# Queries of one batch: from TensorE transposes to a crossbar DMA, and its scores later in the order

## The chip, the cores and the metric

The kernel runs on one core of one Trainium2 chip. The metric is device time in microseconds (us), from launch to end; smaller is better. A core has five engines with an instruction queue each: PE (TensorE, matrix products), DVE (VectorE), ACT (ScalarE), POOL (GpSimd) and SP (SyncE, which here only issues DMAs). An engine takes its instructions strictly in order, so one that waits holds up all behind it. Sixteen DMA engines move data for all of them. In a profile, PEld is PE's loading of weights, and SPq or POOLq is an engine's own queue of DMA issues.

## The reference

Two stages, on 8 batches of 8 heads, with 576 positions of 64 values in each head, and 32 memory slots.

```
a       = softmax(phi) over the 576 positions          # (8, 8, 576, 32)
k_m     = a^T k,   v_m = a^T v                         # 32 slots of 64 values per head
attn    = softmax(q k_m^T / sqrt(64)) over the 32 slots
x       = attn v_m, heads side by side                 # (4608, 512)
out     = (silu(x w_gate) * (x w_val)) w_out           # w_gate, w_val: 512 x 1536; w_out: 1536 x 512
```

Inputs and the output are fp32; the kernel works in bf16 with fp32 sums.

## The kernel before

**Tiling.** A batch is worked on as a whole. Its k and v come as one tile of 128 partitions (two heads side by side, 64 partitions each), its queries as a tile `t_q` of 128 x 2304, which has to be transposed, as 18 blocks of 128 x 128, into `t_qT` before scores can be made. `attn v_m` is never formed: `v_m` is multiplied into the gate and value weights (`U`, lines 453 to 492), and the attention `A` is multiplied by that (`gv_slots`).

**One batch.** Its steps are: exponentials of phi on ACT (`phi_exp`); sums over positions on PE (`kv_items`, L230), whose results DVE scales (`kv_norm`, L266, tile `t_bkv`) and which PE transposes (`kv_T`, L288), with a copy by DVE to `t_kT`; scores on PE (`scores`, L389), which need `t_kT` and `t_qT`, and their exponentials on ACT (L400); the sums of those on DVE (`z_inv_v`) and the scaling by them (`norm`); the products `U` (L465); 24 steps of a gate product, a value product, silu and a multiplication (L508, L525, L531), which give the hidden tile `t_h`.

**The last product.** `h w_out` is done with seven products in place of eight (`products`, line 682): sums and differences of blocks of `h` (tiles `t_S`, made by GpSimd or DVE, `chunk_done`) and of `w_out` (tiles `t_T`, made by DVE, `weight_sums`). A product is six units, and a unit is two matmuls of 128 x 256 (L720) into PSUM. The results are called `first` (12 units), `five`, `six`, `three`, `seven` and `four` (6 each). They share PSUM tiles: `three` adds to the tile of `five` after ACT has copied that out (`keep`, L745). Finished blocks are added up on DVE (L750), and SP stores them (`store_block`, L676).

**Order.** The order of the instructions on each engine is written by hand, as the order of the calls in the program. Batches 0 and 1 run first, while the weights arrive. Then a loop runs over batches 2 to 7. In it, a list `backlog` holds product units of the batch before, and `run(take(6))` puts six of them between two steps of the current batch. For batch 2, `zero` and `one` are the unit lists of batches 0 and 1.

**Queries.** Batches 0, 1 and 2 are transposed on PE (`q_items`, `q_T`, L376: six blocks to a PSUM tile, then a copy to `t_qT` by ACT, L330, or DVE). Batches 3 to 7 go through the crossbar of the DMA engines (`load_qT`, L117), issued by SP: for batch 3 at the head of the loop's first pass, for the later ones near the end of the pass before. `t_q` has two buffers, for even and odd batches; `t_qT` has two as well.

**Loads.** Nearly all loads are issued by GpSimd, between its own additions, and go through one queue in order. A load waits for the eighth load before it to have landed. The order around the change is: weights of the value side (L138), first and second third of `w_out` with k of 2 and phi of 2 between, last third of `w_out` (L153), v of 2 (L103). Then GpSimd makes the `t_S` sums of batch 0, first third, and after them issues phi of 3 and q of 2 (`beside_sums`, line 665); after the sums of batch 1, first third, q of 3; after the next, k and v of 3. `loads(4)` follows near 72 us.

The lines that the change touches, and those around them:

Of the kernel before, what the change touches and what calls it, by code (L numbers as in the profile page):

```python
# [14 lines left out]
def kernel(  # L15
# [19 lines left out]
    nc = tc.nc  # L35
# [39 lines left out]
    def bank(shape, dtype, name):  # L75
        tag = free.pop(0)
        t = ps.tile(shape, dtype, tag=tag, name=name)
        held[id(t)] = tag, t
        return t
# [8 lines left out]
    def head_pairs(x):  # L88

        return x.rearrange("h s d -> (h s d)").rearrange("(i p f) -> p i f", i=NP, p=128)  # L90

    def load_phi(b, eng):
        t = inp.tile([128, NP, JK * M], FP32, tag="phi", name="t_phi")
        eng.dma_start(out=t, in_=head_pairs(phi[b]))
        phis[b] = t
# [6 lines left out]
    def load_v(b):  # L102
        nc.gpsimd.dma_start(out=kvs[b][:, 1], in_=head_pairs(v[b]))  # L103

    def load_q(b):

        t = inp.tile([128, NS * 128], BF16, tag=f"q{Q_SLOT[b]}", bufs=1, name="t_q")
        nc.gpsimd.dma_start(  # L108
            out=t,
            in_=q[b].rearrange("h s d -> (h s d)").rearrange("(p f) -> p f", p=128),  # L110
        )
        qs[b] = t

    def load_qT(b):

        qTs[b] = att.tile([128, NS, 128], BF16, tag="qT", name="t_qT")
        nc.sync.dma_start_transpose(out=qTs[b], in_=qs[b])  # L117
# [33 lines left out]
    def load_wo(c):  # L151
        t = wpool.tile([128, 4, DM], BF16, tag=f"WO{c}", name=f"WO{c}")
        nc.gpsimd.dma_start(  # L153
            out=t,
            in_=moe_w_out[c * CH:(c + 1) * CH, :].rearrange("(i p) f -> p i f", p=128),
        )
        for i in range(4):
            WO[4 * c + i] = t[:, i]
        WOc[c] = t
# [62 lines left out]
    def kv_sum(b, p, parts):  # L222


        w0, w1 = parts[0], parts[-1] + 1
        n = (w1 - w0) * D
        for j in range(JK):
            for i in range(NP):
                for g in range(NG):
                    nc.tensor.matmul(  # L230
                        p[g][32 * i:32 * i + 32, 0:n],
                        lhsT=phi_of(b, g, j, i),
                        rhs=kvs[b][64 * g:64 * g + 64, w0:w1, i, j * D:(j + 1) * D],
                        start=(j == 0),
                        stop=(j == JK - 1),
                        tile_position=(64 * g, 32 * i),
                    )

    def kv_denominators(b, p):

        if b in masked:
            for g in range(NG):
                for j in range(JK):
                    nc.tensor.matmul(
                        p[:, g:g + 1],
                        lhsT=masked[b][:, j, g].rearrange("p i m -> p (i m)"),
                        rhs=ones1,
                        start=(j == 0),
                        stop=(j == JK - 1),
                    )  # L250
            return
        if b in esums:
            hl = esums.pop(b)
            terms = [hl[:, t] for t in range(2)]
        else:
            terms = [ephis[b][:, j].rearrange("p i m -> p (i m)") for j in range(JK)]
        for n, x in enumerate(terms):
            nc.tensor.matmul(p, lhsT=x, rhs=ones2, start=(n == 0), stop=(n == len(terms) - 1))
# [33 lines left out]
    def kv_items(b, beside=None):  # L292


        def run_sums():
            o = 2 * D
            p = [bank([128, CH], FP32, f"p_kv{g}") for g in range(NG)]
            behind = b in esums
            if not behind:
                kv_denominators(b, p[0][:, o:o + NG])  # L300
            kv_sum(b, p, (0, 1))
            if behind:
                beside()
                kv_denominators(b, p[0][:, o:o + NG])
            kv_reciprocal(b, p[0][:, o:o + NG])
            kv_norm(b, p)
            if beside and not behind:
                beside()

        return [run_sums, lambda: kv_T(b)]  # L310
# [329 lines left out]
    def quad_sums(qd):  # L640
# [22 lines left out]
                    subtract(nc.gpsimd, t[:, 2], A12, t[:, 1])  # L663

    beside_sums = {
        (0, 0): lambda: (load_phi(3, nc.gpsimd), load_q(2)),
        (1, 0): lambda: load_q(3),
        (0, 1): lambda: (load_k(3), load_v(3)),
    }
# [1 line left out]
    def store_block(t_o, b, n, cols):  # L671

        rows = out_r[b, n, 0:256, cols].rearrange("(u t) c -> t u c", u=2)
        parts = [slice(u, u + 1) for u in range(2)] if b < 2 else [slice(0, 2)]
        for u in parts:
            nc.sync.dma_start(out=rows[:, u], in_=t_o[:, u, cols])  # L676

# [144 lines left out]
    def q_items(b, evac):  # L822
        return [lambda n=n: q_T(b, n, evac[n]) for n in range(3)]
# [17 lines left out]
    def run(items):  # L841
        for x in items:
            x()
# [10 lines left out]
    def exp_tables():  # L854
        nc.scalar.preload_act_table_set("natural_log_exp_and_others")
# [50 lines left out]
    load_wo(1)  # L906
    load_phi(2, nc.gpsimd)
    load_wo(2)
    load_v(2)
    for c in range(NCH):  # L910
        u_buffer(1, c, f"S{c}")
# [55 lines left out]
    def take(n):  # L967
        nonlocal backlog
        n = max(0, min(n, len(backlog)))
        part, backlog = backlog[:n], backlog[n:]  # L970
        return part
# [17 lines left out]
    for b in range(2, B):  # L989
        last = b + 1 == B  # L990
        exp_tables()
        if b == 2:
            load_qT(3)
            phi_exp(2)
            (zero, ops0), (one, ops1) = products(0, ("c11",)), products(1, ("p1", "c11"))
            kv, q2 = kv_items(2), q_items(2, "aaa")
            run(zero[:6])
            sums = {n: f for n, f in zip(((1, 1), (0, 2), (1, 2)), late)}
            late.clear()
            sums[0, 2]()  # L1000
            weight_sums(0)
            weight_sums(1)
            run(zero[6:12] + one[:6] + kv[:1] + q2[:2])
            weight_sums(2, (0, 1))
            run(zero[12:16] + zero[18:22] + kv[1:] + q2[2:] + zero[16:18] + zero[22:24])
            weight_sums(2, (2, 3))
            ops0["c11"]()
            ops1["p1"]()
            wait_for(Ts[2][0:1, 3, 0, 0:1])
            for part in ((0, 1), (3,), (2,)):  # L1010
                for c in (1, 2):
                    sums[1, c](part)
            loads(4)
            backlog = one[6:12] + zero[36:] + one[12:36]
            ops = ops1
        else:
            run(take(6))
        for g in range(NG):
            scores(b, g)
        if b > 2:  # L1020
            ops["p1"]()
            u_values(b)
        else:
            run(zero[24:36] + take(6))
        run(take(6))
        z_inv_v(b, 0)
        ops["c11"]()
        run(take(6))
        if not last:
            phi_exp(b + 1)  # L1030
        z_inv_v(b, 1)
        if b > 2:
            norm(b, 0)
            norm(b, 1)
        run(take(6))
        run_late()
        if b == 4:
            wait_for(atts[4, 1][0:1, 0, 0:1])
            quad_sums(0)
        nc.scalar.preload_act_table_set("silu_and_others")  # L1040
        run(take(6))
        if b == 2:
            norm(2, 0)
        run(take(6))
        if b == 2:
            norm(2, 1)
            u_three(2)
            run(one[36:])
        g = gv_slots(b)
        quad = []  # L1050
        if b == 4:
            quad = products(b, (), 0)[0]
        if last:
            rest, rest_ops = products(b, (), 1)
            backlog += rest[:12]
        beside = 0 if last else 2 if quad else min(4, len(backlog))
        outs = [lambda: run(take(1)) for _ in range(len(backlog) - beside)]
        streams = [(g, 0, 24), (quad[:12], 0, 3), (quad[12:], 12, 18.5)]
        streams += [(outs, 4, 7 if quad else 24)]
        if b == 2:  # L1060
            streams += [([lambda: u_values(2)], 2.5, 3)]
        if last:
            streams += [([u_item(b, 2)], 5, 6)]
        if not last:
            if b > 2:
                load_qT(b + 1)
            if b > 2 and b != 4:
                phi_sum(b + 1)
            streams += [
                (kv_items(b + 1, lambda: (u_item(b, 2, "aava")(), run(take(2)))), KV, KV + 4),  # L1070
                ([lambda: (u_three(b + 1), run(take(2)))], 19, 20),
            ]
        spread(*streams)
        flush_mul()
        units, ops = products(b, ("p1", "c11"))
        backlog += units
# [34 lines left out]
```

The softmax here doesn't subtract the row's maximum and nothing guards it: scores larger than these inputs give would overflow.

## Time and profile before

| | |
|---|---|
| median of 3 runs | 233.49 us (233.4 to 233.51) |
| profiled execution, device time | 233.53 us |
| its span, first to last instruction | 231.7 us |
| PE, DVE, ACT, POOL busy | 222.8, 185.3, 171.7, 140.6 us |
| TensorE clock granted | 1.00 throughout |
| SP's 5 crossbar transposes of queries, issue to landing | 6.2 to 10.8 us, median 9.5 |
| q of 2: issued, landed | 42.70, 59.1 us |
| v of 2: issued, landed | 34.76, 54.3 us |
| q of 3: issued, landed | 48.20, 61.8 us |
| transposes of q of 2 on PE | from 59.13 and from 61.72 us |
| scores of 2, scores of 3 on PE | 63.11, 92.68 us |

The profile shows one execution. In a list of instructions the columns are start, length, engine, source line, operation, tile written <- tiles read, shape, count. In the chain of work that ended last they are start, length and what ran, followed back from the end. In a table of stretches, each engine's busy time is followed by its count of instructions, and the last three columns are the TensorE clock, the busy share of the DMA engines and the GB/s written. "To landing" is the time from a DMA's issue until its data is there.

### The profile page before, as it was taken

The page shows a single profiled execution, that of the slowest core. Times are in us where ns is not written, and L with a number is a line of the kernel's source. Part 1 is how long each engine was busy: PE and PEld are TensorE (multiplying, and loading weights), DVE is VectorE, ACT ScalarE, POOL GpSimd, SP SyncE. Part 2 cuts the span into 40 slices and gives each one's busy share as a digit, 9 for nine tenths or more (in the row PEclk, how much of TensorE's full clock was granted, in tenths as well). Part 3 has the DMA queues.
Part 4 walks back from the last instruction along what each step waited for, and adds up shares of the span by engine and source line. Part 5 has one row for each costly group of instructions (what it writes and reads, how often), then busy time and mean ns, then how long its engine had stood idle before and what let it go on. Part 6 is the DMA issues. An engine that isn't in the chain of part 4 may idle for free.

```text
span 231.7 us, 7206 instructions
## 1 busy us (share of the span) xinstructions
PE 222.8 (96%) x2825; PEld 169.9 (73%) x2825; DVE 185.3 (80%) x423; ACT 171.7 (74%) x365; POOL 140.6 (61%) x190
## 2 busy tenths in 40 slices
PE   7997899999999999999999999999999999999993
PEld 2554576778887776878788787887788778878882
DVE  4056789999966699989997668998999899977732
ACT  2858998988547889968896658978898789677310
POOL 8422427998199059765977689464845394039291
PEclk9999999999999999999999999999999999999999
DMA  6999999999997992999199945995013502202125
GB/s 211 210 211 205 199 207 207 219 247 269 203 205 197 260 254 44 227 212 183 54 218 193 235 131 104 249 237 102 22 71 106 112 0 95 91 6 88 29 87 160
DMA packets 36674, 36.84 MB, mean 159 GB/s; under 512 B 14624, under 2 KB 31008, under 8 KB 36640
## 3 DMA queue, kind: packets, MB, share of 16 engines
q0 software_dynamic: 16272, 22.42, 52.5%
q1 hardware_dynamic: 19600, 13.18, 22.9%
q10 hardware_dynamic: 768, 0.79, 1.1%
q8 instruction: 22, 0.36, 0.6%
q14 instruction: 12, 0.10, 0.1%
HBM read 42.47 MB, written 9.44 MB: 224 GB/s over the span
## 4 chain that ended last, share of the span: by engine, by line
PE 86%; DMA 9%; POOL 2%; ACT 1%; issue 0%; DVE 0%; POOLq 0%
PE p_g L508 21%; PE p_os L720 21%; PE p_v L508 20%; PE p_oc L720 10%; DMA W<-in_moe_w_val_dram 9%; PE p_oa L720 5%; PE p_u L465 5%; PE p_kv L230 2%; PE p_g L389 1%; POOL t_kv L99 1%; POOL t_kv L103 1%; PE p_q L376 0%; POOL t_q L108 0%; ACT t_qT L330 0%; POOL W L138 0%
## 5 line engine op out<-in xcount | busy, mean ns | idle before, releaser
L531 DVE TENSOR_TENSOR t_h<-t_sg,p_v 128x288 bf16<-128x288 bf16 x192 | 82.0, 452 | 13.7 <-PE p_v L508 6.6
L508 PEld LDWEIGHTS <-t_U 128*128 128x128 bf16 x768 | 73.7, 98 | 21.6 <-issue 3.3
L525 ACT ACTIVATE t_sg<-p_g 128x288 bf16<-128x288 f32 x192 | 73.4, 423 | 17.3 <-PE p_g L508 11.4
L508 PE MATMUL p_g<-t_A,t_U 128*128 128x288 bf16 x384 | 77.0, 286 | 0.0
L508 PE MATMUL p_v<-t_A,t_U 128*128 128x288 bf16 x384 | 77.0, 286 | 0.0
L720 PEld LDWEIGHTS <-t_S 128*128 128x128 bf16 x384 | 37.5, 98 | 4.5 <-issue 0.2
L596 POOL TENSOR_TENSOR t_S<-t_h 128x512 bf16<-128x512 bf16 x17 | 19.6, 1156 | 32.9 <-DVE t_h L531 31.4
L720 PEld LDWEIGHTS <-t_h 128*128 128x128 bf16 x288 | 27.1, 98 | 8.6 <-issue 5.0
L485 ACT CAST t_U<-p_u 128x512 bf16<-128x512 f32 x51 | 27.0, 605 | 6.6 <-PE p_u L465 6.6
L720 PE MATMUL p_os<-t_T,t_S 128*128 128x256 bf16 x192 | 23.7, 273 | 0.0
L553 POOL TENSOR_TENSOR t_S<-t_S,t_h 128x512 bf16<-128x512 bf16 x17 | 19.6, 1154 | 1.3
L553 POOL TENSOR_TENSOR t_S<-t_h 128x512 bf16<-128x512 bf16 x16 | 18.4, 1151 | 0.0
L553 POOL TENSOR_TENSOR t_S<-t_h,t_S 128x512 bf16<-128x512 bf16 x16 | 18.4, 1151 | 0.0
L465 PE MATMUL p_u<-W,t_kT 64*32 64x512 bf16 (+1 forms) x416 | 15.3, 363 | 0.9 <-DVE t_kT L332 0.6
L868 PE MATMUL p_warm<-bones 128*128 128x512 bf16 x44 | 13.7, 452 | 1.7 <-DVE bones L890 1.7
L489 DVE CAST t_U<-p_u 128x512 bf16<-128x512 f32 x21 | 13.6, 684 | 1.9 <-PE p_u L465 1.9
L720 PE MATMUL p_os<-t_T,t_h 128*128 128x256 bf16 x96 | 14.8, 273 | 0.0
L445 DVE TENSOR_TENSOR t_A<-t_E,t_lz 128x576 bf16<-128x576 bf16 x16 | 11.4, 739 | 0.7 <-ACT t_lz L421 0.7
L720 PE MATMUL p_oc<-t_T,t_S 128*128 128x256 bf16 x96 | 12.0, 272 | 0.0
L720 PE MATMUL p_oa<-WO,t_h 128*128 128x256 bf16 x96 | 11.8, 273 | 0.0
L720 PE MATMUL p_oc<-WO,t_S 128*128 128x256 bf16 x96 | 11.8, 272 | 0.0
L720 PE MATMUL p_os<-WO,t_h 128*128 128x256 bf16 x96 | 11.8, 273 | 0.0
(106 smaller groups left out, 308.4 us busy)
## 6 DMA issues: line engine op xcount, KB each, us to landing
out_dram<-t_o SPq DMA_DIRECT2D x11, 512.0 KB, 3.1
t_kv<-in_k_dram POOLq DMA_DIRECT2D x8, 576.0 KB, 10.7
t_q<-in_q_dram POOLq DMA_DIRECT2D x8, 576.0 KB, 8.6
t_kv<-in_v_dram POOLq DMA_DIRECT2D x8, 576.0 KB, 14.8
t_phi<-in_phi_dram POOLq DMA_DIRECT2D x6, 576.0 KB, 8.2
out_dram<-t_o SPq DMA_DIRECT2D x10, 256.0 KB, 3.8
WO<-in_moe_w_out_dram POOLq DMA_DIRECT2D x3, 512.0 KB, 19.2
W<-in_moe_w_gate_dram POOLq DMA_DIRECT2D x2, 512.0 KB, 16.3
```

The lines of the kernel that those rows point to most:

```text
L230: nc.tensor.matmul(p[g][32 * i:32 * i + 32, 0:n], lhsT=phi_of(b, g, j, i), rhs=kvs[b][64 * g:64 * g + 64, w0:w1, i, j * D:(j + 1) * D], st ...
L445: nc.vector.tensor_tensor(out=a, in0=es.pop((b, g)), in1=lzs.pop((b, g)), op=ALU.mult)
L465: nc.tensor.matmul(p[g][32 * i:32 * i + 32, o:o + n], lhsT=kTs[b][64 * g:64 * g + 64, 2, 32 * i:32 * i + 32], rhs=w_part(w, c, i, g, halve ...
L485: nc.scalar.copy(out=t, in_=p)
L489: nc.vector.tensor_copy(out=t, in_=p)
L508: nc.tensor.matmul(p[:, 0:HALF], lhsT=Us[b, c, g][:, o // 2, which, 128 * (o % 2):128 * (o % 2 + 1)], rhs=atts[b, g][:, r], start=(g == 0) ...
L525: nc.scalar.activation(out=sg, in_=gate[:, 0:HALF], func=AF.Silu)
L531: nc.vector.tensor_tensor(out=dst, in0=sg, in1=val[:, 0:HALF], op=ALU.mult)
L553: eng.tensor_tensor(out=out, in0=x, in1=y, op=ALU.subtract)
L596: eng.tensor_tensor(out=t[:, 0], in0=A21, in1=A22, op=ALU.add)
L720: nc.tensor.matmul(mine[home][:, u], lhsT=lhs(c, m, u), rhs=rhs(c, m), start=fresh and u == 0, stop=(k == 5), skip_group_check=u == 1 or n ...
L868: nc.tensor.matmul(p[:, 0:128 * a], lhsT=bones, rhs=x.to_broadcast([128, a, 128]) if a > 1 else bones, start=True, stop=True,)
```

## The change

1. The queries of batch 2 are no longer loaded after GpSimd's first sums but ahead of v of batch 2, as the last load but one before those sums.
2. They are transposed by the crossbar, issued by SP at the head of the loop's first pass, in the place that batch 3's had. The 18 PE transposes and the three ACT copies go. Batch 3's transpose is issued near the end of that pass, like those of later batches.
3. The scores of batch 2 come after 18 product units (`zero[24:36]` and the first six of `backlog`) that came after them before.
4. Batch 1's blocks are stored with one DMA each, not two.

```diff
     beside_sums = {
-        (0, 0): lambda: (load_phi(3, nc.gpsimd), load_q(2)),
+        (0, 0): lambda: load_phi(3, nc.gpsimd),
...
-        parts = [slice(u, u + 1) for u in range(2)] if b < 2 else [slice(0, 2)]
+        parts = [slice(u, u + 1) for u in range(2)] if b < 1 else [slice(0, 2)]
...
     load_phi(2, nc.gpsimd)
     load_wo(2)
+    load_q(2)
     load_v(2)
...
         if b == 2:
-            load_qT(3)
+            load_qT(2)
             phi_exp(2)
             (zero, ops0), (one, ops1) = products(0, ("c11",)), products(1, ("p1", "c11"))
-            kv, q2 = kv_items(2), q_items(2, "aaa")
+            kv = kv_items(2)
...
-            run(zero[6:12] + one[:6] + kv[:1] + q2[:2])
+            run(zero[6:12] + one[:6] + kv[:1])
             weight_sums(2, (0, 1))
-            run(zero[12:16] + zero[18:22] + kv[1:] + q2[2:] + zero[16:18] + zero[22:24])
+            run(zero[12:16] + zero[18:22] + kv[1:] + zero[16:18] + zero[22:24])
...
-        else:
-            run(take(6))
+            run(zero[24:36])
+        run(take(6))
         for g in range(NG):
             scores(b, g)
         if b > 2:
             ops["p1"]()
             u_values(b)
-        else:
-            run(zero[24:36] + take(6))
         run(take(6))
...
         if not last:
-            if b > 2:
-                load_qT(b + 1)
+            load_qT(b + 1)
```

## The prediction

> **What bounds the kernel now.** I read the page first: busy shares, then the chain of work that ended last.
>
> ```profile
> span 231.7 us, 7206 instructions
> PE 222.8 (96%) x2825; PEld 169.9 (73%) x2825; DVE 185.3 (80%) x423; ACT 171.7 (74%) x365; POOL 140.6 (61%) x190
> PE 86%; DMA 9%; POOL 2%; ACT 1%; issue 0%; DVE 0%; POOLq 0%
> ```
>
> PE sets the end; the DMA part of the chain is the weights' load before 26.7 us. So a wait of PE after that costs its whole length, and work taken from PE gains only where PE doesn't wait at once for something else. Next I read the chain around the change (start, length, work).
>
> ```profile
> 58.46 0.73 PE p_kv L230 x72
> 59.19 0.78 PE p_q L376 x12
> 59.97 0.87 PE p_oc L720 x8
> 60.84 0.87 PE p_os L720 x8
> 61.72 0.17 PE p_T L288 x3
> 61.88 0.35 PE p_q L376 x6
> ...
> 63.06 0.50 ACT t_p L745
> 63.55 0.04 issue
> 63.59 1.47 PE p_oc L720 x12
> ```
>
> Here stand the 18 query transposes, and the 0.7 us of scores and wait ahead of the product at 63.59. What could take over when they go is on DVE (its timeline):
>
> ```profile
> 60.17 0.99 DVE L266 TENSOR_SCALAR t_bkv<-p_kv,t_rS 128x128 bf16<-128x128 f32 x4
> 61.08 0.41 DVE L553 TENSOR_TENSOR t_T<-WO 128x512 bf16<-128x512 bf16 x1
> 61.53 0.42 DVE L553 TENSOR_TENSOR t_T<-WO,t_T 128x512 bf16<-128x512 bf16 x1
> ```
>
> Last I read the crossbar transposes in the view of tile t_qT, and the DMA share and GB/s (last two columns) around the first of them, which is issued at 61.85.
>
> ```profile
> L117 SPq DMA_TRANSPOSE t_qT<-t_q x5: 3986/6003/7322, 61.9 to 177.0; - x5
> DMA to landing us min/median/max: 6.2/9.5/10.8
> ```
>
> ```profile
> 62.00:64.00 2.00, 1.94 (x32) 1.43 (x30) 1.55 (x4) 1.74 (x4) 0.99 (x2) 1.00 1.21 208
> 64.00:65.00 1.00, 1.00 (x11) 0.90 (x10) 0.00 (x0) 1.00 (x5) 0.92 (x2) 1.00 1.21 207
> 65.00:67.00 2.00, 2.00 (x21) 1.78 (x20) 1.28 (x2) 0.75 (x3) 1.92 (x3) 1.00 1.28 150
> 67.00:68.00 1.00, 1.00 (x12) 0.90 (x10) 0.97 (x3) 0.00 (x0) 1.00 (x2) 1.00 1.30 139
> 68.00:69.00 1.00, 1.00 (x12) 0.90 (x10) 0.97 (x3) 0.00 (x0) 1.00 (x2) 1.00 1.27 289
> ```
>
> The engines run at 207 GB/s, the rate of GpSimd's casting loads, until 65, and at the transpose's own 289 GB/s only at 68: it hardly moves while loads are queued. The landings, each from its issue and time to landing, say the same. Transposes issued at 61.85, 100.73 and 124.36 land at 71.35, 110.4 and 135.2; the last loads then queued land at 67.8, 105.8 and 131.4, so 3.6 to 4.6 us before them. Only the one at 177.02, with no load queued, lands in 6.2.
>
> The single DMA records give the rule. A transpose is 2304 pieces of 256 bytes, 144 on each of 16 engines. The first record of the one issued at 61.85 is at 65.25, 4 ns after the first engine's last record of the load of v of batch 3. On the engine that loads longest, value rows come 88 ns apart before; then they stand at 66.869, 66.983, 67.097, 67.211: 114 ns apart, with one 256-byte piece between each two. So an engine with both kinds queued gives one piece per row, at 26 ns more. Such turns begin on the slow engines at about 65.9, 4.05 us after issue. The last loading row ends at 67.55, the last piece is at 69.37, the landing at 71.35. Where other engines ran ahead, pieces stall 0.1 to 1.5 us, so the slowest engine sets the pace.
>
> [...] turns are of one row and one 256-byte piece (and from 79 to 84 us, beside stores, of about 93 rows and 90 store pieces a us). [...] 69.37 to 71.35 is 2.0. [...]
>
> **The change part by part.**
>
> *Transposes off PE, scores moved.* By the starts of their neighbours, the 18 transposes take 59.13 to 59.81 and 61.72 to 62.06: 1.02 us. Without them:
> - Units of five and six start at 59.13; PE is ready for the key transposes (p_T) at 60.87, but t_bkv ends at 61.16 on a DVE that is unchanged. They start at 61.3, not 61.55.
> - The next units need the T tiles of 61.49 and 61.95; they end at 62.43, not 62.92.
> - Product three needs ACT's copy of p_oc (0.59 us). Before, this stood behind a query copy until 62.95; now it starts at 62.25, so three starts at 62.85, not 63.59. Three query copies (0.80 each) leave ACT: no gain beyond this, as ACT isn't the bound.
> - 18 units of 2 matmuls, 1.31 us per six, bring PE to the scores at 62.85 + 3.93 = 66.8. The scores cost 0.26 (92.68 to 92.94 in batch 3) and about 0.2 for the steps into and out of their tile shape. The next product starts at 67.3, not 67.52. Gain if the scores find their queries: 0.2 us.
>
> *Queries of batch 2 loaded earlier.* On GpSimd a load waits for the eighth before it to land. Queries take the values' place at 34.76; the values then wait for the next weight load, landing at 21.52 + 15.6 = 37.1. GpSimd's first sums start at 37.9, not 37.0, and one load fewer follows (0.55), so the later ones are 0.3 late: hidden, since PE wants them at 59 and they end at 53.4. If that cover were gone it would cost 0.3. In the queue the values land one load later: 54.3 becomes 57.1 (2.8 us a load). PE wants them at 58.4: hidden by 1.3 us, each us beyond costs one.
>
> *The crossbar on batch 2.* Queries land at 54.2 (the values' old place), SP is idle, so the transpose is issued there. Queued on the engines then: values of 2, phi of 3, queries of 3, and k and v of 3 (issued 53.7 to 55.3), ending at 67.15 on the slowest engine had it no turns. Turns begin at 54.2 + 4.05 = 58.3. From there that engine has about 2 rows of phi, 8 of queries (0.34 us each), 32 of keys, 32 of values: 74 turns, which cost 74 x 0.026 = 1.9 us, so loads end at 69.1. The other 144 - 74 = 70 pieces take 14 ns each: 70.1. [...] landing is at **72.1**. Bounds: no turn before the loads end (67.15 + 2.0 + 2.0 = 71.2); turns earlier, some 90 (72.4); none of the loads in its way (54.2 + 6.2 = 60.4).
> PE, in order, stands at the scores from 66.8 to 72.1: **5.3 us**. Behind it are every later product and the gate matmuls. The exponentials, z and norm follow as much later; DVE, which idled 1.76 us ahead of its copy at 73.03, takes the order.
>
> *Queries of batch 3 on the crossbar later.* No longer at 61.85 but behind batch 1's last store, 77.26 plus the 5.1 lost: about 82.5. The loads of 4, queued from 73 to 89, and stores are ahead; landing 91 to 93. Scores of 3 want it at 92.7 + 5.1 = 97.8, and GpSimd's load of q 5, which reuses the buffer, at 91.5 + 5.1. Hidden; without the 5.1 the margin would be 0 to 2 us.
>
> *Stores.* Batch 1's go as one DMA per block: same bytes, two SP issues fewer. Batch 0's no longer stand behind the transpose of 3 but behind that of 2: released about 69, not 67.9. Nobody waits: nothing.
>
> Sum: -0.2 + 5.3 = +5.1. On its own time: 231.7 + 5.1 = 236.8 span, plus the 1.8 around it (233.53 - 231.7) = **238.6 us**. That execution lies 0.04 from the median.
>
> **Rivals.**
> - *The transfer is hidden* (not slower): the engines take pieces 16 at a time[...]: 9 turns beside the queries' rows (9 x 0.57 = 5.1), so 58.3 + 5.1 + 2.0 = 65.4 and no wait: 233.3. It decides where landing is before 66.8, 12.6 us after issue; no transpose here took over 10.8, which speaks for it, but none had 13 us of loads queued. The 114 ns rhythm speaks against.
> - *Strict order*, the transpose last: 71.2, so +4.2: 237.7. The idle start until 65.25 speaks for it, the turns on slow engines against.
> - *The values become the wait*: landing later than 58.4. With 2 us more than my 57.1, PE loses 0.7 there: 234.0 if alone, little beside the later wait. Loads landing every 2.8 us speak against.
> - *Half way*: turns that favour the transpose, landing 68 to 70.5: 234.5 to 237.
>
> **How the numbers follow.** Forecast, landing 71.6 to 73: 0.66; strict order 0.14; half way 0.08; hidden 0.09; values 0.03. The forecast's own range is 238.0 to 239.6. Taking in strict order and reserve above, for turns that cost more or a start that is later, gives 237.0 to 239.7, which leaves out the 0.2 of the last three. A gain over 0.2% (0.47 us; less can't be told from no change) would need more than the 0.2 found: 0.02. Within: most of hidden, 0.08. Slower: 0.90.
>
> **What would show it.** The page: no p_q for batch 2; PE waiting for DMA t_qT for some 5 us near 67; the transpose issued at 54 with over 16 us to landing; values landing near 57 with no wait at L230; GpSimd's first sum at 37.9. I am wrong if the transpose lands within 12.6 us, or if PE waits at L230, or if scores of 3 wait too.

## The result, and the profile after

The changed kernel takes **239.01 us** (median of 6 runs, 238.62 to 240.17) against 233.46 of the kernel before on the same chip: ratio 1.0244, 95% interval 1.0223 to 1.0265. The forecast was 238.6. Its profiled execution took 239.27 us, with a span of 237.5 us (before: 231.7).

The page of the kernel after: span, busy times, clock row of the 40 slices (each 5.9 us), shares of the chain that ended last.

```profile
span 237.5 us, 7168 instructions
PE 224.0 (94%) x2807; PEld 169.7 (71%) x2807; DVE 185.7 (78%) x423; ACT 169.5 (71%) x362; POOL 140.6 (59%) x190
PEclk9999999999997999999999999999999999999998
PE 79%; DMA 15%; POOL 2%; DVE 1%; issue 1%; POOLq 0%
```

PE has 18 matmuls fewer and yet 1.2 us more of busy time, and one slice has a clock of 7. DMA has gone from 9% to 15% of the chain. The view of tile t_qT says which DMA:

```profile
L117 SPq DMA_TRANSPOSE t_qT<-t_q x6: 3616/6962/11779, 54.3 to 182.7; - x6
DMA t_qT<-t_q: 3.9, 1
DMA to landing us min/median/max: 7.1/10.5/16.7
```

One transpose needs 16.7 us to land, where the longest before needed 10.8, and PE waits for it once. The timeline of PE around it (start, length, work; in brackets the idle time before it and what ended that):

```profile
61.48 0.34 PE L288 MATMUL p_T<-ident,t_bkv 128*128 128x128 bf16 x3 [0.62 <-DVE t_bkv L266]
...
63.08 1.47 PE L720 MATMUL p_oc<-WO,t_S 128*128 128x256 bf16 x12 [0.21 <-ACT t_p L745]
...
65.70 1.47 PE L720 MATMUL p_oa<-WO,t_h 128*128 128x256 bf16 x12
71.12 0.29 PE L389 MATMUL p_g<-t_qT,t_kT 64*32 64x288 bf16 x1 [3.95 <-DMA t_qT<-t_q]
...
71.49 2.03 PE L720 MATMUL p_os<-t_T,t_h 128*128 128x256 bf16 x12
73.31 2.64 PE L720 MATMUL p_oc<-t_T,t_S 128*128 128x256 bf16 x12
75.79 1.47 PE L720 MATMUL p_os<-t_T,t_S 128*128 128x256 bf16 x12
```

PE reaches the scores of batch 2 at 67.17 and waits 3.95 us. That was forecast. What was not: the next two groups of 12 matmuls take 2.03 and 2.64 us, where such a group takes 1.47. The stretches of 1 us say why (the third column from the right is the granted clock):

```profile
71.00:72.00 1.00, 0.88 (x21) 0.61 (x22) 0.00 (x0) 0.50 (x2) 1.00 (x2) 1.00 0.77 295
72.00:73.00 1.00, 1.00 (x8) 0.78 (x7) 0.76 (x1) 0.82 (x3) 1.00 (x2) 0.64 0.00 0
73.00:74.00 1.00, 1.00 (x7) 0.69 (x6) 0.93 (x3) 0.44 (x1) 1.00 (x3) 0.50 0.50 46
74.00:75.00 1.00, 1.00 (x6) 0.71 (x5) 1.00 (x3) 0.14 (x1) 1.00 (x2) 0.50 0.64 78
75.00:76.00 1.00, 1.00 (x8) 0.76 (x6) 0.93 (x3) 0.00 (x0) 0.27 (x1) 0.66 1.05 194
76.00:77.00 1.00, 1.00 (x12) 0.89 (x10) 0.50 (x1) 0.96 (x2) 0.00 (x0) 1.00 1.14 194
```

From 72.3 to 75.7 PE has half its clock: 0.36 + 0.50 + 0.50 + 0.34 = 1.70 us of work lost. The first gate product (L508) then starts at 82.00; before, at 76.35. The two timelines of PE, after and before:

```profile
82.00 0.65 PE L508 MATMUL p_g<-t_A,t_U 128*128 128x288 bf16 x4
```

```profile
76.35 0.65 PE L508 MATMUL p_g<-t_A,t_U 128*128 128x288 bf16 x4
```

Of these 5.65 us, 3.95 are the wait and 1.70 the clock; the other effects on PE cancel. From there on the two kernels run alike: the span is 5.8 us longer.

Two things were left to be shown: that the loads queued beside it make the transpose late, and that PE's idle time costs the clock. A third came up on the way.

### The profile page after: what moved, and what is told of

It is laid out like the page before. It is cut to its first block, busy times and chain, and to the rows that moved or that the text cites. A ratio compares the mean times of both kernels' runs of the same rounds, so it can differ in the third digit from the quotient of the medians.

```text
span 237.5 us, 7168 instructions
## 1 busy us (share of the span) xinstructions
PE 224.0 (94%) x2807; PEld 169.7 (71%) x2807; DVE 185.7 (78%) x423; ACT 169.5 (71%) x362; POOL 140.6 (59%) x190
## 4 chain that ended last, share of the span: by engine, by line
PE 79%; DMA 15%; POOL 2%; DVE 1%; issue 1%; POOLq 0%
PE p_g L508 20%; PE p_v L508 19%; PE p_os L720 18%; PE p_oc L720 9%; DMA W<-in_moe_w_val_dram 8%; DMA t_qT<-t_q 7%; PE p_u L465 5%; PE p_oa L720 4%; PE p_kv L230 2%; DVE t_h L531 1%; PE p_g L389 1%; POOL t_kv L99 1%; POOL t_kv L103 1%; POOL t_q L108 0%; POOL W L138 0%
## 5 line engine op out<-in xcount | busy, mean ns | idle before, releaser
L508 PEld LDWEIGHTS <-t_U 128*128 128x128 bf16 x768 | 73.7, 98 | 21.6 <-issue 3.5
L508 PE MATMUL p_g<-t_A,t_U 128*128 128x288 bf16 x384 | 77.0, 286 | 0.0
L508 PE MATMUL p_v<-t_A,t_U 128*128 128x288 bf16 x384 | 77.0, 286 | 0.0
L720 PEld LDWEIGHTS <-t_S 128*128 128x128 bf16 x384 | 38.1, 100 | 5.5 <-issue 0.4
L720 PE MATMUL p_os<-t_T,t_h 128*128 128x256 bf16 x96 | 15.4, 281 | 0.0
L428 DVE TRANSPOSE_TENSOR_REDUCE t_z<-t_E 128x18 f32<-128x576 bf16 x12 | 9.2, 765 | 5.7 <-ACT t_E L400 5.7
L720 PE MATMUL p_oc<-t_T,t_S 128*128 128x256 bf16 x96 | 13.1, 290 | 0.0
L745 ACT COPY t_p<-p_oc 128x512 f32<-128x512 f32 (+1 forms) x10 | 5.4, 543 | 10.0 <-PE p_oc L720 10.0
```

What stands on the lines that cost most here:

```text
L428: nc.vector.tensor_reduce(out=z[:, 0], in_=es[b, g].rearrange("p r (n t) -> p (r n) t", t=32), axis=mybir.AxisListType.X, op=ALU.add, appl ...
L508: nc.tensor.matmul(p[:, 0:HALF], lhsT=Us[b, c, g][:, o // 2, which, 128 * (o % 2):128 * (o % 2 + 1)], rhs=atts[b, g][:, r], start=(g == 0) ...
L720: nc.tensor.matmul(mine[home][:, u], lhsT=lhs(c, m, u), rhs=rhs(c, m), start=fresh and u == 0, stop=(k == 5), skip_group_check=u == 1 or n ...
```

## The experiments

Each is an edit of the changed kernel.

**The loads in the way of the transpose (two runs).** My theory: each row of a load queued on a DMA engine lets one 256-byte piece of the transpose through, so fewer queued loads mean an earlier landing. Against it: the transpose is simply slow or late, whatever is queued. The first edit loads keys and values of batch 3 later, the second only the values.

```diff
-        (0, 1): lambda: (load_k(3), load_v(3)),
...
                     sums[1, c](part)
+                    if part == (0, 1) and c == 1:
+                        load_k(3)
+            load_v(3)
             loads(4)
```

> The changed kernel, but k of batch 3 is loaded after four of the late sums of batch 1 (near 66 us, not 54), and v of 3 ahead of the loads of batch 4 (near 73, not 55). Theory (the crossbar pieces take turns, one for one, with the rows of loads queued on the same engines): only phi and q of 3 are then in its way, about 10 turns on an engine, and the other 134 pieces at 14 ns each follow the end of q of 3 near 61.5. Landing near 64.5, no wait of PE at the scores, which it reaches near 67.2; time 233.5, the other edits being worth -0.2 to +0.3. Rival (the place of the scores, or the store and load edits, cost the time): still 238 to 239. Rival (the crossbar takes 16.7 us whatever is queued): still 239.

```diff
-        (0, 1): lambda: (load_k(3), load_v(3)),
+        (0, 1): lambda: load_k(3),
...
+            load_v(3)
             loads(4)
```

> The changed kernel, with only v of batch 3 loaded later (ahead of the loads of batch 4). Theory of turns: k of 3 is still in the way, about 42 turns on an engine; loads end near 64.3 + 42 x 0.026 = 65.4 on the slowest engine, the other 102 pieces take 1.4 us, and landing is near 67.4 with the 0.6 us that the changed kernel showed after its last piece. PE waits 0.2 to 0.5 us: 233.7 to 234.0. Rival (crossbar last in strict order): landing near 64.3 + 2.0 + 0.6 = 66.9, no wait: 233.5, which this run can hardly tell from turns. Rival (a fixed time, or another edit): 239.

(In the first, the keys stand behind two of the late sums, not four: they are issued at 64.87.) The place in question did as the theory says. In the single DMA records the pieces of the transpose end at 70.48 in the changed kernel, at 66.73 with late values and at 63.30 with late keys and values. PE's wait at the scores goes from 3.95 to 0.35 to nothing; the gates start at 82.00, 76.58 and 75.57. But the times are 239.29 us (1.0219, 1.0194 to 1.0243) and 238.38 us (1.0192, 1.0174 to 1.0210): the forecasts of the times failed. The timelines of PE show where it went. With late keys and values, and then with late values alone:

```profile
83.04 1.16 PE L230 MATMUL p_kv<-t_kv,t_ephi 64*32 64x128 bf16 x72 [3.48 <-DMA t_kv<-in_v_dram]
```

```profile
67.37 0.29 PE L389 MATMUL p_g<-t_qT,t_kT 64*32 64x288 bf16 x1 [0.35 <-DMA t_qT<-t_q]
...
96.04 0.42 PE L389 MATMUL p_g<-t_qT,t_kT 64*32 64x288 bf16 x1 [3.06 <-DMA t_qT<-t_q]
```

The first is the edit's own fault: values of 3, issued at 72.5, were late. The second is not: it is the transpose of batch 3, whose place the change also moved. In both runs the clock falls to 0.50 again after PE has gone idle. So the theory of the turns stands (a transpose strictly behind the loads would have ended nearly as late in these two runs; the counts of rows and pieces, given in the part on the prediction, speak against it). And a second victim has shown itself: once PE is not held up at 67, the transpose of batch 3 is the late one. SP's timeline of the run with late values:

```profile
54.38 8.93 SPq L117 DMA_TRANSPOSE t_qT<-t_q  x1
65.22 12.65 SPq L676 DMA_DIRECT2D out_dram<-t_o  x6
77.99 12.93 SPq L117 DMA_TRANSPOSE t_qT<-t_q  x1
```

It is issued at 77.99, with four loads of batch 4 and stores ahead, and lands at 96.0.

**The crossbar undone for batch 2.** All else of the change is kept.

```diff
-            load_qT(2)
...
-            kv = kv_items(2)
+            kv, q2 = kv_items(2), q_items(2, "aaa")
...
-            run(zero[6:12] + one[:6] + kv[:1])
+            run(zero[6:12] + one[:6] + kv[:1] + q2[:2])
...
-            run(zero[12:16] + zero[18:22] + kv[1:] + zero[16:18] + zero[22:24])
+            run(zero[12:16] + zero[18:22] + kv[1:] + q2[2:] + zero[16:18] + zero[22:24])
```

> The changed kernel, but the queries of batch 2 are transposed on PE and copied by ACT, as before the change; their earlier load, the scores behind 18 units, the later transpose of batch 3 and the merged stores stay. Theory (all of the loss is the crossbar's landing and what follows from it): no wait at the scores, 18 transposes back; 233.5 to 233.9, of which 0 to 0.3 is GpSimd's later load and its effect on DVE. Rival (moving the scores or the load costs by itself): 235 or more.

235.94 us (1.0099, 1.0070 to 1.0128). No wait at the scores of 2, gates at 76.72, and yet 2.1 us slower than before. Its timelines of SP and of PE:

```profile
78.14 10.36 SPq L117 DMA_TRANSPOSE t_qT<-t_q  x1
```

```profile
94.04 0.29 PE L389 MATMUL p_g<-t_qT,t_kT 64*32 64x288 bf16 x1 [0.92 <-DMA t_qT<-t_q]
```

The same late transpose of batch 3, landing at 94.0. Of the 1.8 us that this profiled execution is longer than the one before, 0.37 stand at the gates and 0.92 here; PE's weight loads also wait 0.6 once for the DMA of t_kT. So the change loses 2.15 us with batch 2's transposes on PE and 5.55 with them on the crossbar. The difference, 3.4, is what this transpose adds; it is less than PE's wait for it and the clock (5.65), because that wait hides batch 3's late transpose in the changed kernel. To test that reading, the transpose of batch 3 was put back at the head of the loop:

```diff
+            load_qT(3)
             phi_exp(2)
...
-            load_qT(b + 1)
+            if b > 2:
+                load_qT(b + 1)
```

> The run with the query transposes of batch 2 back on TensorE, and besides the crossbar transpose of batch 3 back at the head of the loop, where the kernel before has it. What is left of the change: queries of batch 2 loaded ahead of its values, scores of 2 behind 18 more units, batch 1 stored in one DMA per block. Theory (the 2.1 us that the run without the head's transpose still lost came from batch 3's own transpose, issued at 78.1 and landed at 94.0): it is issued near 62 again and lands by 72, scores of 3 do not wait, and the time is before plus the 0.37 us by which the gate products stood later there (76.72 against 76.35): 234.2 us (233.8 to 234.6, where before is 233.8). Rival (the loss is of the loads, the stores or the longer wait for the scores): it stays near 235.9.

234.12 us (1.0013, 0.9998 to 1.0028), as expected: it is issued at 61.34 and nobody waits for it (SP's timeline):

```profile
61.34 5.96 SPq L117 DMA_TRANSPOSE t_qT<-t_q  x1
```

Against 233.65 for the kernel before on its chips 0.47 us are left, so 1.7 of the 2.15 us come back. What is left of the change here (queries loaded ahead of values, scores 18 units later, stores joined) costs at most 0.3%.

**What the wait itself costs.** PE gets 16 products of 128 x 512, whose results nobody reads, in the place where it would be idle.

```diff
         run(take(6))
+        if b == 2:
+            warm(64)
         for g in range(NG):
             scores(b, g)
```

> The changed kernel with 16 idle products of 128x512 put on PE just ahead of the scores of batch 2, about 3.4 us of its wait of 3.95; their results are not used. Theory (after the wait the clock granted to PE is lower for some us, which makes the next 24 matmuls 1.7 us longer): with PE kept busy the clock stays at 1.00 and those matmuls take 1.31 us per 12 again: 237.3 to 237.5. Rival (the slow matmuls wait for something else, such as DVE's or GpSimd's late results, or share a resource with the DMAs): 239.0, as without the products. If the products push the scores back, up to 0.3 is added to either.

237.93 us (1.0188, 1.0161 to 1.0215): 4.1 us above the kernel before on its chip (233.79), where the changed kernel is 5.5 above, though the scores start as late. The timeline of PE and the clock of the same run:

```profile
67.26 3.62 PE L868 MATMUL p_warm<-bones 128*128 128x512 bf16 x16
71.15 0.29 PE L389 MATMUL p_g<-t_qT,t_kT 64*32 64x288 bf16 x1 [0.27 <-DMA t_qT<-t_q]
...
71.52 1.48 PE L720 MATMUL p_os<-t_T,t_h 128*128 128x256 bf16 x12
72.84 1.47 PE L720 MATMUL p_oc<-t_T,t_S 128*128 128x256 bf16 x12
...
80.36 0.65 PE L508 MATMUL p_g<-t_A,t_U 128*128 128x288 bf16 x4
```

```profile
72.00:73.00 1.00, 1.00 (x12) 0.90 (x10) 0.72 (x1) 0.85 (x3) 1.00 (x2) 1.00 0.09 16
73.00:74.00 1.00, 1.00 (x12) 0.90 (x10) 0.93 (x3) 0.58 (x1) 1.00 (x2) 1.00 0.00 0
```

The groups are back at 1.47 and the clock at 1.00; the gates start at 80.36, 1.64 earlier. That the idle time costs the clock is shown by this pair (0.50 for 3.4 us after 3.95 us of idle PE, 1.00 after 0.27); the rival, that the products after the wait are slow for another reason, falls. The time is 0.4 us above the upper end of what was expected. One of the four executions took 239.48 us at a mean clock of 0.989, about what one such stretch of half clock costs; it has no profile, so it isn't shown that the products keep the clock every time.

**The place of the scores (two runs).** First where the kernel before has them, then behind 12 more units than in the changed kernel.

```diff
-            run(zero[24:36])
-        run(take(6))
+        else:
+            run(take(6))
         for g in range(NG):
             scores(b, g)
+        if b == 2:
+            run(zero[24:36] + take(6))
```

> The changed kernel with the scores of batch 2 at the place that they had before the change, ahead of the 18 units. Theory (landing is fixed by the DMA queues at about 71.0, whatever PE does): PE waits from about 62.7 to 71.1, and the 18 units follow after it: 239.0 + 3.9 = 242.9, and up to 1 more if the clock recovers more slowly after a longer wait. Rival (the later place of the scores delays the work behind them and is itself part of the loss): 239 or less.

```diff
-            run(zero[24:36])
+            run(zero[24:36] + take(12))
```

> The changed kernel with the scores of batch 2 behind 12 units more (30, not 18). Theory: PE reaches them at 67.2 + 2.6 = 69.8, waits 1.3 us for a landing that stays at 71.0, and the kernel gains 2.6: 236.4. If the lower clock after the wait comes only with a wait longer than that, another 1.7 is gained: 234.7. Rival (the exponentials, sums and scaling of batch 2 become late for its gate products, which start 24 units after the scores before and 12 after them here): 237 to 239.

At the old place: 243.64 us (1.0417, 1.0392 to 1.0442), within what was expected. PE waits 8.05 us and gets half the clock from 64.8, while it still waits, to 75.1:

```profile
71.00 0.40 PE L389 MATMUL p_g<-t_qT,t_kT 64*32 64x288 bf16 x1 [8.05 <-DMA t_qT<-t_q]
```

So the 18 units are worth 4.3 us as a cover (9.8 above before without them, 5.5 with them). Twelve further back: 236.71 us (1.0119, 1.0102 to 1.0135). PE waits 1.34 us, the clock stays at 1.00, and the clock's 1.7 us are gone, but the time expected for that, 234.7, is not reached. The timeline of PE shows the price:

```profile
71.16 0.29 PE L389 MATMUL p_g<-t_qT,t_kT 64*32 64x288 bf16 x1 [1.34 <-DMA t_qT<-t_q]
...
77.77 1.47 PE L720 MATMUL p_os<-t_T,t_h 128*128 128x256 bf16 x12 [1.36 <-DVE t_o L750]
```

DVE has its sums of the exponentials ahead of the additions L750; with the scores as late as 71, these come late, and PE waits for them. More cover in PE's order doesn't help when DVE's work hangs on the scores too.

**Both transposes out of the way of the loads (five runs).** With the two causes known, a placing was looked for in which neither transpose is late. In all five `load_qT(3)` leaves the end of the pass, as above. First: values of 3 behind GpSimd's second late sum, both transposes at the head.

```diff
-        (0, 1): lambda: (load_k(3), load_v(3)),
+        (0, 1): lambda: load_k(3),
...
             load_qT(2)
+            load_qT(3)
...
                     sums[1, c](part)
+                    if part == (0, 1) and c == 1:
+                        load_v(3)
```

> The whole change, with two things besides: values of 3 are loaded after GpSimd's first two late sums (near 65.5) rather than at 55.2, so that the transpose of 2 has less in its way, and the transpose of 3 is issued at the head of the loop, right behind that of 2. Theory: the transpose of 2 lands near 67.7 as in the run with late values, so PE waits 0.2 to 0.5 us there; that of 3 starts when queries of 3 and the one ahead are done, lands by 76 and is waited for by nobody; gates start near 76.6 (before: 76.35) and the time is 234.0 us (233.7 to 234.4). Rival one: batch 0's stores, now behind two transposes on SP's queue (72 rather than 68), free their tiles late and PE waits for a buffer: 235 to 236. Rival two: the loss lies elsewhere than in the two transposes: about 238.

236.74 us (1.0149, 1.0116 to 1.0183): its first rival, and a little above the 235 to 236 put on it. The scores wait 0.32 us, as forecast, but batch 0's stores, behind two transposes in SP's queue, go out at 68.09 and land late. In the timelines of DVE and of PE:

```profile
77.67 0.69 DVE L750 TENSOR_TENSOR t_o<-p_os,t_p 128x512 f32<-128x512 f32 x1 [2.76 <-DMA out_dram<-t_o]
```

```profile
78.42 2.72 PE L720 MATMUL p_os<-t_T,t_h 128*128 128x256 bf16 x12 [2.89 <-DVE t_o L750]
```

DVE waits for the tile that a store still reads, PE for DVE; and in this execution (238.7 us) 2.89 us of idle PE are enough for half a clock (2.72 us for the 12 matmuls). Four of the six executions, 236.1 to 237.0 us at a mean clock of 0.998, kept the clock. Second: the same, with `load_qT(3)` behind `run(zero[24:36])`, so that two stores go ahead of it.

> As the last, but the transpose of 3 stands on SP's queue behind the first two stores of batch 0 (issue near 67) rather than ahead of them. Theory: it starts near 67 to 71 beside the loads of 4, lands by 84, before scores of 3 want it at 93, so about the same 234.0 us (233.6 to 234.6), with batch 0's first stores early and its later ones and batch 1's behind the transpose. Rival: the later stores, held until about 78, hold up their tiles: 235 to 236.

233.94 us (1.0020, 1.0010 to 1.0029), as expected. Third: keys late as well, `load_qT(3)` where the second has it, to win the 0.8 us that the run with both late had shown at the gates.

```diff
-        (0, 1): lambda: (load_k(3), load_v(3)),
...
                     sums[1, c](part)
+                    if part == (0, 1):
+                        (load_k if c == 1 else load_v)(3)
```

> The whole change with its loads and transposes placed by what the runs have shown: keys of 3 loaded between GpSimd's late sums (near 65.5) and values of 3 two sums later (near 68.5), and the transpose of 3 on SP's queue behind batch 0's first two stores. Theory: the transpose of 2 meets only queries of 3 and lands before 64, PE reaches the scores at 66.4 without a wait, and the gates start at 75.6, as in the run with late keys and values (75.57; before: 76.35). That run lost it again because values of 3 were loaded at 72.5 and the transpose of 3 was issued at 77.0; here values land by 78, before their products at 80, and the transpose of 3 before 90. So 233.65 - 0.8 = 232.9 us (232.6 to 233.4), ratio 0.997. Rival: keys and values now share the engines with the transpose of 3 and the loads of 4, and the stores of batch 0 behind it or values of 3 come late: 234.5 to 236.5.

245.52 us (1.0506, 1.0481 to 1.0531): far outside both theories. The timeline of PE, and the stretches of 2 us ahead of it (last column: GB/s):

```profile
89.27 1.16 PE L230 MATMUL p_kv<-t_kv,t_ephi 64*32 64x128 bf16 x72 [9.15 <-DMA t_kv<-in_v_dram]
```

```profile
74.00:76.00 2.00, 1.99 (x36) 1.37 (x36) 1.93 (x4) 1.51 (x4) 2.00 (x3) 1.00 1.55 79
76.00:78.00 2.00, 2.00 (x23) 1.29 (x21) 1.25 (x4) 2.00 (x7) 0.14 (x1) 1.00 1.44 119
78.00:80.00 2.00, 2.00 (x25) 1.63 (x23) 1.32 (x4) 2.00 (x6) 0.00 (x0) 1.00 1.48 81
```

The transpose of 3, keys and values of 3 and the loads of 4 share the engines: 79 to 119 GB/s, where loads alone have about 207. In the single DMA records rows and pieces go in turn, as before, but at 30 to 90 of each per us from 75 to 90; in the changed kernel it was 143 and 144 from 67 to 68. The turns alone give no such rate; what slows both is open.

Fourth: the transposes at the head and the loads after them, so that they hardly meet (keys behind GpSimd's fourth late sum, values behind all eight).

```diff
-        (0, 1): lambda: (load_k(3), load_v(3)),
...
             load_qT(2)
+            load_qT(3)
...
+                    if part == (0, 1) and c == 2:
+                        load_k(3)
+            load_v(3)
             loads(4)
```

> The whole change, keys and values of 3 late (keys after GpSimd's fourth late sum, near 67.2; values behind all eight, at 72.5, ahead of the loads of 4), and both transposes at the head of the loop, where now no load but queries of 3 is in their way. The last run showed that a transpose beside queued loads slows both (80 to 144 GB/s), so that values of 3 came at 88; here transposes and loads hardly meet. Theory: the transpose of 2 lands near 64 and that of 3 by 69, batch 0's stores go out at 66 and land ahead of the keys, values land near 78, before their products at 80; no wait at the scores, gates at 75.6 (before: 76.35), so 233.65 - 0.8 = 232.9 us (232.6 to 233.4), ratio 0.997. Rival: something is late again, the values at 80 (each us beyond costs one) or a tile of batch 0's stores: 234 to 236.

237.75 us (1.0185, 1.0149 to 1.0222). Both transposes are through at 66.78 and the gates start at 75.77, but values of 3 are late once more, by 3.00 us:

```profile
82.76 1.16 PE L230 MATMUL p_kv<-t_kv,t_ephi 64*32 64x128 bf16 x72 [3.00 <-DMA t_kv<-in_v_dram]
```

Fifth: the same with keys and values of 3 behind the second and the fourth late sum.

> As the last, with keys of 3 behind GpSimd's second late sum (near 64.9) and values of 3 behind the fourth (near 68.1), so that the values are ahead of the loads of 4 by 5 us. In the last run both transposes were through at 66.8, batch 0's stores at 68.1, and the gates started at 75.77; only values of 3, issued at 72.7, landed at 82.3 and cost 3.0 us and some clock. Theory: values land near 77, before their products at 80; the two loads between the sums hold GpSimd's last sums up as in the run with the transpose of 3 in the middle (0.4 us there), so gates near 75.9 against 76.35 before: 233.5 - 0.4 = 233.1 us (232.8 to 233.6), ratio 0.998. Rival: keys at 64.9 meet the second transpose's last pieces and batch 0's stores come late, or values are late still: 234.5 to 237.

233.58 us against 233.73 (0.9997, 0.9988 to 1.0005), the upper part of what was expected, and no measurable gain. SP's and PE's timelines:

```profile
54.31 10.63 SPq L117 DMA_TRANSPOSE t_qT<-t_q  x2
65.00 35.65 SPq L675 DMA_DIRECT2D out_dram<-t_o  x7
```

```profile
62.34 1.47 PE L719 MATMUL p_oc<-WO,t_S 128*128 128x256 bf16 x12 [0.24 <-ACT t_p L744]
73.37 0.61 PE L719 MATMUL p_os<-t_T,t_S 128*128 128x256 bf16 x4 [0.35 <-POOL t_S L553]
80.33 0.80 PE L230 MATMUL p_kv<-t_kv,t_ephi 64*32 64x128 bf16 x72 [0.27 <-DMA t_kv<-in_v_dram]
```

The scores start at 66.36 without a wait. But 0.35 us go to GpSimd's sums, behind two more load issues, so the gates start at 76.07, 0.28 ahead of before, and the values take 0.27 of that: scores of 3 stand at 92.7, as before. The crossbar for batch 2 is thus not slower in itself: it costs nothing measurable where keys and values of 3 are not queued beside it. A version that beats the kernel before was not found.

## Why the prediction was right, point by point

The mechanism of the wait was right: turns of rows and pieces. That the time is within half a us was luck, as errors nearly cancel: the wait was 1.35 us shorter than worked out, 1.70 us of clock were not in the sum, and a gain of 0.2 did not come (5.1 - 1.35 + 1.70 + 0.2 = 5.65).

- *Landing of the queries and start of the turns.* Worked out: issue at 54.2, turns from 58.3, loads' end at 69.1, last piece at 70.1. Measured in the DMA records: 54.34, 58.38, 69.09, 70.48. From 60 to 68 us the loads' rows and the 256-byte pieces go one to one (102 and 109, 101 and 106, 141 and 133 in the first three us; 921 and 941 in all). The two runs with later loads agree at two other points (last piece worked out near 66.8 and 63.4, measured 66.73 and 63.30). It is also what rules out the rivals: the rival's sixteen pieces per turn would have ended near 63.4, and a transpose behind all loads could hardly have moved 941 pieces beside 921 rows.
- *From the last piece to the landing.* The 2.0 us added there came from the one transpose of the profile before that was measured so (69.37 to 71.35); here it is 0.6 (70.48 to 71.08), with late values 0.5, with late keys and values 2.0 again. This is the larger part of the wait's error. Why it differs is open.
- *PE at the scores.* Worked out 66.8, measured 67.17. The step that failed is "later sums 0.3 late: hidden". GpSimd's sums are 0.6 late (keys of 3 issued at 54.36, before at 53.73), since its values' load waited until 37.42. Its copies to t_x (L585) then still run when DVE makes the first t_T, which takes 0.64 us in place of 0.41; t_bkv ends at 61.42, not 61.16. The copies end at 57.44 and that t_T starts at 57.08; in the run with PE's transposes it is 57.40 and 57.04, and 0.64 again. Where the t_T starts after the copies (57.05 after 56.84 before, 56.99 after 56.78 in the second of the five placings), it takes 0.41. That the copies slow DVE is the author's reading of this; no run isolates it. So the forecast gain of 0.2 is lost.
- *The wait.* 5.3 worked out, 3.95 measured: landing 1.0 earlier, PE 0.4 later.
- *The clock.* No step of the sum had it, and the profile before, at 1.00 throughout, does not show it. In the runs the half clock lasts 3.4 us here and with late values, at least 6.5 with late keys and values (82.0 to 88.5). The shortest idle stretch that was followed by it is 2.89 us.
- *The values.* Landing 57.4 (worked out 57.1), no wait at L230: as forecast, and that rival falls.
- *The transpose of batch 3.* "Hidden" held in the changed kernel: it lands at 95.2, the scores want it at 98.3. But landing was put at 91 to 93, and the margin without the stall, "0 to 2 us", was wrong in sign: in the run with late values PE waited 3.06 us for it, and in the run with PE's transposes it cost 1.7 of 2.15 us. The stall at 67 was its cover. An edit costed at nothing because another one holds PE up is no free edit; its price comes due when the other is mended.
- *Stores, scores moved.* Nothing, as forecast, within the 0.3% of the run that keeps only these and the loads' order. SP was free for batch 0's stores at 66.17, where about 69 was worked out: its own queue is done with the transpose at 66.1, before that lands (71.08).

## What to carry to other kernels

In four cases here a crossbar transpose issued while loads were queued landed soon after the last of those loads: 3.6 to 4.6 us after it in three of the profile before, 1.1 in the changed kernel (71.08, where values of 3, issued at 55.13, took 14.9). So ask which loads stand on the engines then, and move them or it, before counting what the compute engine saves. When a stall is forecast, price the clock with it (here 1.70 us on a wait of 3.95, nothing on one of 1.34), and go through every edit that was costed at nothing because of that stall. A repair can move the wait to the next transfer in line (here 3.95 us at the scores of 2 became 0.35 there and 3.06 at the scores of 3), so each placing has to be followed to the one after.

## What the runs showed of the hardware

- After one idle stretch of PE of 2.89, 3.00, 3.06, 3.48, 3.95, 8.05 or 9.15 us (seven profiled runs) the clock fell to 0.50; after 1.34 and, 5 us later, 1.36 it did not. It fell between 1.9 us (in the run with the scores at the old place) and 5.1 us (in the changed kernel) after PE had gone idle, so also when work had begun again.
- By the stretches of 1 us, the half clock lasted 3.4 us in four of these runs, at least 6.5 in the one with late keys and values, and 10.2 in the two with the longest waits. It did not come in every execution: four of six kept the clock with values late and both transposes at the head (236.1 to 237.0 us, mean clock 0.998 to 0.999), and one of six in the run with 3.00 us of wait (235.99 us, mean clock 1.00). These five have no profile. What sets the length, and which idle stretches cost the clock, is not shown.
- In one run transposes and loads together moved less than their turns give: with five or six loads beside one transpose 79 to 119 GB/s from 74 to 80 us, and PE waited 9.15 us for a load. In the changed kernel the keys and values of 3 beside one transpose moved 190 to 214 GB/s from 65 to 69 us; what makes the difference is open.
